# Storing x of the first three batches as one float32 plane and splitting it at its first use in the feed-forward part

## The chip, the cores and the metric

One core of a Trainium2 chip runs the whole program. The time is device microseconds of one execution. The kernel before was timed in three runs: 839.45, 842.1 and 845.86 us, median 842.1 us.

## What is computed

Attention over 4 batches, 12 heads, 448 positions and head size 64, whose scores and whose weights are mixed across the heads, and behind it a feed-forward part with a rational function:

```python
scores = scale * np.matmul(q, k.transpose(0, 1, 3, 2))
scores = np.einsum('bhij,hg->bgij', scores, w_pre)
attn = softmax(scores)
attn = np.einsum('bhij,hg->bgij', attn, w_post)
x = np.matmul(attn, v)          # as [1792 tokens, 768]
h = x @ w_in                    # w_in [768, 2048]
g = (a0 + a1*h + a2*h*h + a3*h**3) / (1 + |b0|*|h| + |b1|*h*h + 1e-6)
out = g @ w_out                 # w_out [2048, 768]
```

All inputs are float32 but for w_in and w_out, which are float64.

## The kernel before

**Attention** goes by 16 tiles of query rows, four a batch (three of 120 rows and one of 88). A tile is worked off in 6 groups (the short one in 5). For each group TensorE mixes the heads of the scores (L565, into the PSUM pair ps_t or ps_u), VectorE takes the maximum (nm, L571), ScalarE the exponential (e, L580), GpSimd and VectorE make the reciprocal of the sum (sm, rr) and GpSimd scales the second mixing matrix by it (krs, L600), TensorE mixes with that (L640, ps_a) and VectorE transposes the result (aa, L656). Between the groups TensorE makes the scores of the next tile (L496). These are copied (st, L236 on ScalarE or L238 on VectorE) and rearranged by DMA into the buffer d (L512). When all groups of a tile are through, `put_av` multiplies with v in three steps (L705) into whichever of the pairs ps_t and ps_u the groups do not use at that time; the pair is named `holds[T]`.

**What leaves attention.** After the third step, for each of the two halves hv of that pair, ScalarE copies it to Xs in the rounded matmul type (`hi`, L236, plane 0), and VectorE subtracts that from PSUM (`lo`, L723, plane 1). The two planes together carry float32 precision. The pair is free after `lo`. The planes of a batch lie in one SBUF tile `xs` (two halves, two planes, three blocks of 448 columns) and are stored to `x_scr[b]` in eight pieces (L728): four after the third tile of a batch, four after the fourth. There is one such SBUF tile, so the next batch's first `hi` waits for the stores.

**Feed-forward** goes by 64 units of one block of 128 hidden columns and one batch, in four rounds of four blocks. The first matmuls of a unit (L879, 18 of them, into ps_s) take x and the first half of W, twelve elementwise operations on ScalarE and VectorE (L892 to L929) make g, which is split in two planes (`hi` L236 or L238, `lo` L939 on GpSimd or VectorE), and 18 second matmuls (L969) add it into six PSUM banks. The float64 weights are decoded on the way (L405 to L449: ScalarE cm, GpSimd cm L415, VectorE cm and cg, ScalarE and GpSimd w L446), one piece per unit. Batches come in the order 0, 3, 1, 2 in the first round. Batch 3 is used from Xs; all others, and all later uses, are loaded from `x_scr` by `put_load_x` (L860), one DMA of 2688 KB, either into the buffer d of attention or into `xs`. The first of them (batch 0) can start when the last but one tile of attention has let go of d.

**What sets the order.** Every operation is given to `Plan` with a duration, a wished time `at` and its dependencies; `Plan.run` is a list scheduler that fixes the order of the instructions of each engine and of SP's DMA queue, and for operations that may run on two engines also which one takes it. So a change in a few operations moves many others. Each engine then works its list in order.

Of the kernel before, what the change touches and what calls it, by code (L numbers as in the profile page):

```python
# [9 lines left out]
F32 = mybir.dt.float32  # L10
F32R = mybir.dt.float32r
# [7 lines left out]
B, H, S, D = 4, 12, 448, 64  # L19
# [9 lines left out]
NT = 4 * B  # L29
# [3 lines left out]
KD = DM // 128  # L33
NF = DFF // 128
CH = 8
PH = 4
# [18 lines left out]
class Plan:  # L55
# [140 lines left out]
def dve(n, fast=False):  # L196
    return 0.16 + 0.53e-3 * n if fast else 0.14 + 1.06e-3 * n
# [14 lines left out]
ON = {  # L212
    "q_hi": ('act', 'dve'), "q_lo": ("dve", "pool"), "k_hi": ('act', 'dve'), "k_lo": ('dve', 'pool'), "w_hi": ('act',), "w_lo": ("pool",),
    "s": ('act', 'dve'), "d_hi": ('act', 'dve'), "d_lo": ("dve", "pool"), "p": ("act", "dve"), "x_hi": ("act",),
    "g_hi": ("act", "dve"), "g_lo": ("dve", "pool"),
}


def dma(nbytes):
    return nbytes / 300e3  # L220
# [21 lines left out]
def mixed_attention_then_rational_ffn(ctx: ExitStack, tc, q, k, v, w, wmix, mask, a, b2, out):  # L242
# [3 lines left out]
    nc = tc.nc  # L246
# [5 lines left out]
    add = plan.add  # L252
# [8 lines left out]
    sb = {}  # L261
# [29 lines left out]

    w_scr = [dram.tile([128, 2, WC], F32, name=f"w_scr{f}") for f in range(PH)]
    x_scr = [dram.tile([128, 2, 2, 3, S], F32, name=f"x_scr{b}") for b in range(B)]
    o_scr = [dram.tile([128, KD, S], F32, name=f"o_scr{b}") for b in range(B)]

    SLOT, HALF = 3.65, 2.2
# [2 lines left out]
    UNIT = 7.35  # L299
# [390 lines left out]
    def put_av(T, pr, at):  # L690
# [19 lines left out]
        def part(hv):  # L710
            return box[hv][:, 0:3 * n].rearrange("p (r w) -> p r w", r=3)[:, :, 0:r]

        def hi(hv):
            def fn(eng):
                if hv == 0 and T % 4 == 0:
                    Xs[b] = sb["xs"].tile([128, 2, 2, 3, S], F32R, tag="xs", name="xs")
# [20 lines left out]
        for hv in range(2):  # L737
            deps, after = [o], []
            if hv == 0 and T % 4 == 0:
                deps.append(R["xs"].take())  # L740
            else:
                after.append(xs_op[b][0])
            h_ = add(copies(3 * n, False, on=ON["x_hi"]), 0, hi(hv), deps, at=at, after=after)
            l_ = add("dve", dve(3 * n), lo(hv), [h_], at=at)
            xs_op.setdefault(b, []).append(h_)
            x_done.setdefault((b, hv), []).append(l_)
            R["ps_" + holds[T]].uses[slots[hv].k].append(l_)
            if T % 4 > 1:
                last = T % 4 == 3
                cols, done = (slice(c0, S), x_done[b, hv][3:]) if last else (slice(0, c0 + r), x_done[b, hv][:])  # L750
                for hl in range(2):
                    when = at + (3.0 if last else 5.0) + (1.6 if last else 4.0) * (2 * hl + hv)
                    s_ = bulk(0.45, store(hv, hl, cols), done, at=when, nbytes=128 * 3 * max(cols.stop - cols.start, 240) * 4, late=1.0, since=when - 1.0)
                    x_st.setdefault(b, []).append(s_)
                    R["xs"].uses[b].append(s_)

    xs_op, x_done = {}, {}
    x_st = {}

    LEAD = {1: 15.0, 2: 9.0, 3: 15.0}  # L760
    put_q(0, at=-10.0)
# [61 lines left out]
    x_use = {0: R["xs"].uses[B - 1]}  # L823
    x_ld[0] = x_done[B - 1, 0] + x_done[B - 1, 1]
    o_use, o_st = {}, {}
    m1_op = {}
# [25 lines left out]
    def put_load_x(n, at):  # L852
        b, name = homes[n]

        def fn():
# [4 lines left out]
            nc.sync.dma_start(out=t.bitcast(F32), in_=x_scr[b])  # L860
            X[n] = t
        x_ld[n] = [add(
            "sp", 0.63, fn, [R[name].take(), R["d"].uses[NT - 2] if n == 1 else op_rest, x_st[b]], at=at, extra=dma(128 * 2 * KD * S * 4))]
        x_use[n] = R[name].uses[-1]

    def put_unit(u):
        c, b, f = units[u]
# [172 lines left out]
            for c in range(NCV):  # L1040
                put_w(f, c, at=END1 - 26.0 + 6.0 * c, since=END1 - 40.0 + 6.0 * c, g=len(groups) - 8 + 2 * c)
    for n in homes:
        put_load_x(n, at=END1 + UNIT * PH * (held.index(n) - 1) + 1 if n > 1 else END1 - 45.0)
    for u in range(len(units)):
        i = u + PH * NCV
        if i < NF * NCV:
# [64 lines left out]
```

## Time and profile before

| what | value |
|---|---|
| median of three runs (lowest, highest) | 842.1 us (839.45, 845.86) |
| span of the profiled execution | 837.6 us |
| TensorE busy in the span | 802.3 us, 96% |
| VectorE, ScalarE, GpSimd busy | 684.7, 493.8, 339.4 us |
| mean granted TensorE clock | 0.994 |

The profile is of one more execution. Its span runs from the first to the last instruction; what lies around it is not shown, and the median of the timed runs stands 4.5 us above the span. Attention fills the first 350 us, the two parts overlap until about 372 us, and the rest is the feed-forward part. In the first 60 us attention starts up. Busy time of TensorE is that of its matmuls, which are pipelined; time in which it is not busy is a wait that other views put down to what ended it.

### The profile page before, as it was taken

To read this page: it belongs to the slowest core of one execution; us is meant where nothing else is said; L and a number is where in the kernel's file an instruction comes from. 1 tells how busy PE (TensorE), PEld (TensorE's weight loads), DVE (VectorE), ACT (ScalarE), POOL (GpSimd) and SP (SyncE) were. 2 spreads that over 40 slices of the span, in tenths; PEclk is the share of its full clock that TensorE was granted. 3 is DMA by queue.
4 is the path that set the end of the run, shared out by engine and by line. 5 is a ranking of instruction groups with operands and counts; after the bars stand their busy time and mean duration, and the time that the engine had idled before them with its cause. 6 is when DMAs were issued, how large, how long until landed. Compare 5 with 4: busy or idle time off the path is not lost.

```text
span 837.6 us, 23295 instructions
## 1 busy us (share of the span) xinstructions
PE 802.3 (96%) x9360; PEld 597.7 (71%) x9360; DVE 684.7 (82%) x1177; ACT 493.8 (59%) x1079; POOL 339.4 (41%) x464
## 2 busy tenths in 40 slices
PE   5789999999999999999999999999999999999998
PEld 1244454454444454589989899998999998999997
DVE  5677788788788888889988988999998999866665
ACT  2456667556565566576676665666566566445542
POOL 2224444343444343734555434465445455212111
PEclk8999999999999999999999999999999999999999
DMA  6678788677886775985633255753485544166314
GB/s 203 197 207 225 241 269 250 198 222 239 261 243 202 241 233 157 341 292 204 230 123 100 80 194 209 280 186 101 148 309 186 219 151 151 61 225 242 114 62 154
DMA packets 75355, 166.46 MB, mean 199 GB/s; under 512 B 12944, under 2 KB 52720, under 8 KB 74096
## 3 DMA queue, kind: packets, MB, share of 16 engines
q1 hardware_dynamic: 74648, 164.01, 59.1%
q8 instruction: 74, 1.21, 0.6%
q10 hardware_dynamic: 600, 0.97, 0.4%
q14 instruction: 33, 0.27, 0.1%
HBM read 88.50 MB, written 37.75 MB: 151 GB/s over the span
## 4 chain that ended last, share of the span: by engine, by line
PE 57%; DVE 16%; ACT 3%; issue 3%; POOL 2%; DMA 1%; SPq 0%; ACTq 0%; DVEq 0%; POOLq 0%
PE ps_s L879 19%; PE ps_u L969 6%; PE ps_a L969 6%; PE ps_t L969 6%; PE ps_a L640 5%; PE ps_s L496 5%; PE ps_t L565 3%; PE ps_u L705 3%; PE ps_u L565 2%; PE ps_t L705 2%; DVE cg L424 2%; DVE ua L925 2%; DVE cm L430 1%; DVE nm L571 1%; DVE ua L929 1%
## 5 line engine op out<-in xcount | busy, mean ns | idle before, releaser
L415 POOL TENSOR_SCALAR cm<-cm 128x384 f32<-128x384 f32 x64 | 103.3, 1616 | 46.6 <-ACT cm L410 46.3
L656 DVE STREAM_TRANSPOSE aa<-ps_a 128x448 f32<-128x448 f32 (+1 forms) x184 | 107.7, 617 | 13.7 <-PE ps_a L640 13.2
L939 POOL TENSOR_TENSOR g<-ua,g 128x448 fp32r<-128x448 f32 x47 | 57.8, 1230 | 138.8 <-ACT g L236 73.6
L600 POOL TENSOR_SCALAR krs<-kpost,rr 128x64 f32<-128x64 f32 x180 | 81.5, 466 | 74.3 <-DVE rr L591 54.0
L879 PE MATMUL ps_s<-xs,w 128*128 128x448 f32 x504 | 107.5, 366 | 2.9 <-DVE m L908 2.9
L879 PE MATMUL ps_s<-d,w 128*128 128x448 f32 x504 | 107.5, 366 | 1.3 <-DVE m L908 1.3
L496 PE MATMUL ps_s<-kk,q 64*64 64x448 f32 x720 | 94.4, 553 | 9.2 <-DMA kk<-in_k 5.0
L879 PEld LDWEIGHTS ps_s<-xs,w 128*128 128x128 f32 x504 | 94.4, 188 | 11.9 <-DVE m L908 4.0
L879 PEld LDWEIGHTS ps_s<-d,w 128*128 128x128 f32 x504 | 94.3, 188 | 10.3 <-DVE m L908 1.7
L236 ACT COPY st<-ps_s 120x448 f32<-120x448 f32 (+1 forms) x121 | 60.6, 533 | 68.1 <-PE ps_s L496 33.6
L640 PEld LDWEIGHTS ps_a<-e,krs 64*32 64x32 f32 x2880 | 45.2, 106 | 74.5 <-issue 34.4
L640 PE MATMUL ps_a<-e,krs 64*32 64x224 f32 x2880 | 93.6, 358 | 1.2 <-DVE aa L656 0.6
L446 POOL TENSOR_TENSOR w<-cm,w 128x384 fp32r<-128x384 f32 x48 | 54.7, 1140 | 87.7 <-ACT w L236 87.7
L892 ACT ACTIVATE m<-ps_s,a_sb 128x448 f32<-128x448 f32 x64 | 46.1, 720 | 69.5 <-PE ps_s L879 69.2
L969 PE MATMUL ps_u<-g,w 128*128 128x448 f32 x336 | 83.9, 366 | 0.0
L969 PE MATMUL ps_a<-g,w 128*128 128x448 f32 x336 | 83.8, 366 | 0.0
L969 PE MATMUL ps_t<-g,w 128*128 128x448 f32 x336 | 83.4, 366 | 0.0
L580 ACT ACTIVATE e<-ps_t,nm 128x448 f32<-128x448 f32 x92 | 57.7, 634 | 26.5 <-DVE nm L571 22.4
L587 POOL TENSOR_SCALAR sm<-sm 128x2 f32<-128x2 f32 (+1 forms) x92 | 20.9, 227 | 123.5 <-ACT e L580 121.4
L915 ACT ACTIVATE ua<-sq 128x448 f32<-128x448 f32 x64 | 37.0, 579 | 55.5 <-DVE sq L912 55.1
L580 ACT ACTIVATE e<-ps_u,nm 128x448 f32<-128x448 f32 x88 | 55.2, 634 | 24.0 <-DVE nm L571 20.4
L969 PEld LDWEIGHTS ps_t<-g,w 128*128 128x128 f32 x336 | 63.0, 188 | 5.6 <-DVE g L939 0.3
(89 smaller groups left out, 1516.5 us busy)
## 6 DMA issues: line engine op xcount, KB each, us to landing
d<-st SPq DMA_DIRECT2D x144, 210.0 KB
cr<-in_w SPq DMA_DIRECT2D x64, 384.0 KB
o_scr<-o SPq DMA_DIRECT2D x36, 448.0 KB
o<-o_scr SPq DMA_DIRECT2D x36, 448.0 KB
d<-x_scr SPq DMA_DIRECT2D x5, 2688.0 KB
xs<-x_scr SPq DMA_DIRECT2D x4, 2688.0 KB
d<-st SPq DMA_DIRECT2D x42, 157.5 KB
x_scr<-xs SPq DMA_DIRECT2D x12, 540.0 KB
```

The source lines that it names most:

```text
L236: eng.copy(o, i)
L415: nc.gpsimd.tensor_scalar(out=m, in0=m, scalar1=F64_MIN, scalar2=F64_MAX, op0=ALU.max, op1=ALU.min)
L446: eng.tensor_sub(t[:, 1, :], box["m"].bitcast(F32), t[:, 0, :].bitcast(F32))
L496: nc.tensor.matmul(box["s"][hh][i0:i1, 0:S], lhsT=Q[T][d, pr, i0:i1], rhs=K[b][d, pr, :], start=True, stop=True)
L580: nc.scalar.activation(e, box[r]["t"][:, 0:S], AF.Exp, bias=box[0]["nm"][:, r:r + 1], accum_out=box[0]["sm"][:, r:r + 1])
L600: eng.tensor_scalar_mul(box[r]["kr"], kpost, rr)
L640: nc.tensor.matmul(banks[c]["p"][q_:q_ + BT, JH * r:JH * (r + 1)], lhsT=box[r]["kr"][p, m_, :], rhs=box[r]["e"][p, JH * jh:JH * (jh + 1)], ...
L656: nc.vector.transpose(o, src)
L879: nc.tensor.matmul(h[:, 0:S], lhsT=W[fi][:, wi, kk * 128:(kk + 1) * 128], rhs=x[:, kk // 3, xj, kk % 3, :], start=(n == 0), stop=(n == 3 * ...
L892: nc.scalar.activation(new("m"), box["h"], AF.Identity, scale=a_sb[:, 3:4], bias=a_sb[:, 2:3])
L939: eng.tensor_sub(g[:, 1, :], box["rc"], g[:, 0, :].bitcast(F32))
L969: nc.tensor.matmul(O[key][:, 0:S], lhsT=W[fi][:, wi, DM + m * 128:DM + (m + 1) * 128], rhs=box["g"][:, gi, :], start=(f == 0 and n == 0), ...
```

## The change

For batches 0, 1 and 2 (`whole`), `hi` is a plain float32 copy into Y[b], one half of the same SBUF tile `xs` (the halves take turns by batch), and `lo` is gone, so that the PSUM pair is free after the copy. After the fourth tile Y is stored to a new scratch `y_scr[b]` in six pieces of 224 KB. Batch 3 stays as it was.

At the first use of batches 0, 1 and 2 in the feed-forward part `put_load_x` loads y (two DMAs of 672 KB) into the place of the second plane, ScalarE copies it block by block into the first plane (six copies of 448 columns), VectorE or GpSimd subtracts in place (six), and both planes are stored to `x_scr[b]` (two DMAs of 1344 KB) for the later uses, which load x as before.

```diff
@@ put_av
+        whole = b < B - 1
         def hi(hv):
             def fn(eng):
                 if hv == 0 and T % 4 == 0:
...
+                    if whole:
+                        Y[b] = Xs[0].rearrange("p v l k s -> p (v l) k s").bitcast(F32)[:, 2 * (b % 2):2 * (b % 2) + 2]
-                move(nc, eng, Xs[b][:, hv, 0, :, c0:c0 + r], part(hv))
+                move(nc, eng, Y[b][:, hv, :, c0:c0 + r] if whole else Xs[b][:, hv, 0, :, c0:c0 + r], part(hv))
...
+        def store_y(hv, kk):
+            def fn():
+                nc.sync.dma_start(out=y_scr[b][:, hv, kk], in_=Y[b][:, hv, kk])
+            return fn
...
-            l_ = add("dve", dve(3 * n), lo(hv), [h_], at=at)
+            l_ = h_ if whole else add("dve", dve(3 * n), lo(hv), [h_], at=at)
...
-            if T % 4 > 1:
+            if whole:
+                if T % 4 == 3:
+                    for kk in range(3):
+                        when = at + 3.0 + 1.6 * (3 * hv + kk)
+                        s_ = bulk(0.45, store_y(hv, kk), x_done[b, hv][:], at=when, nbytes=128 * S * 4, late=1.0, since=when - 1.0)
...
@@ put_load_x
+        if b in x_st:
+            x_ld[n] = [add("sp", 0.63, fn, [*free, x_st[b]], at=at, extra=dma(128 * 2 * KD * S * 4))]
+            return
...
+                nc.sync.dma_start(out=X[n][:, hv, 1].bitcast(F32), in_=y_scr[b][:, hv])
...
+                move(nc, eng, X[n][:, hv, 0, kk], X[n][:, hv, 1, kk].bitcast(F32))
...
+                x = X[n][:, hv, 1, kk]
+                eng.tensor_sub(x, x.bitcast(F32), X[n][:, hv, 0, kk].bitcast(F32))
...
+                nc.sync.dma_start(out=x_scr[b][:, hv], in_=X[n][:, hv].bitcast(F32))
...
+        for hv in range(2):
+            got.append(bulk(0.5, load(hv), [*free, y_st[b]], at=at + hv, nbytes=128 * 3 * S * 4, after=got[:1]))
...
+                h_ = add(copies(S, on=ON["x_hi"]), 0, hi(hv, kk), [got[hv]], at=when)
+                parts += [h_, add(subs(S, on=ON["x_lo"]), 0, lo(hv, kk), [h_], at=when)]
...
+            s_ = bulk(0.63, store(hv), parts, at=at + lead + gap * (3 * hv + 3) + 2.0, nbytes=128 * 2 * 3 * S * 4)
```

Three places show how the order moves. The first is VectorE at the end of a tile in attention; xs is x on its way out, rr, nm and aa belong to the groups of the next tile. Before:

```order
L591 RECIPROCAL rr<-sm 128x2
L723 TENSOR_TENSOR xs<-ps_t,xs 128x3x120 x2
L571 TENSOR_REDUCE nm<-ps_u 128x2
L656 STREAM_TRANSPOSE aa<-ps_a 128x2x7x32 x2
```

and with the change, the same place of the same tile:

```order
L592 RECIPROCAL rr<-sm 128x2
L572 TENSOR_REDUCE nm<-ps_u 128x2
L238 COPY st<-ps_s 120x448
```

The two subtractions between rr and nm are gone, and VectorE takes a copy of scores (st) behind nm; over the whole program it has 6 more of these copies than before, and ScalarE 6 fewer.

The second place is ScalarE at the end of attention, from the last copy co of the weights' decoding to the load of the table for the feed-forward part; d is where batch 0 is loaded to. Before:

```order
L236 CAST co<-cm 128x384
L580 ACTIVATE e,sm<-ps_u,nm 128x448 x2
L580 ACTIVATE e,sm<-ps_t,nm 128x448 x2
L580 ACTIVATE e,sm<-ps_u,nm 128x448 x2
L410 ACTIVATE cm<-cr 128x384
L236 CAST w_6258<-cm 128x384
L580 ACTIVATE e,sm<-ps_t,nm 128x448 x2
L236 CAST w_6258<-cm 128x384
L580 ACTIVATE e,sm<-ps_t,nm 128x448 x2
```

and with the change:

```order
L236 CAST co<-cm 128x384
L581 ACTIVATE e,sm<-ps_u,nm 128x448 x2
L236 CAST d<-d 128x448
L581 ACTIVATE e,sm<-ps_t,nm 128x448 x2
L236 CAST d<-d 128x448
L581 ACTIVATE e,sm<-ps_u,nm 128x448 x2
L236 CAST d<-d 128x448
L236 CAST w_6212<-cm 128x384
L411 ACTIVATE cm<-cr 128x384
L236 CAST d<-d 128x448 x2
L581 ACTIVATE e,sm<-ps_t,nm 128x448 x2
L236 CAST d<-d 128x448
```

The six copies of batch 0 stand one by one between the exponentials. The six subtractions behind them stand three on GpSimd, between its sm and krs, and three on VectorE, between two nm.

The third place is SP's queue in the first round of the feed-forward part, between the loads of batch 1 (into d) and of batch 2 (into xs); cr are loads of weights to decode, o_scr stores of partial sums. Before:

```order
L860 DMA d<-x_scr_123 128x5376
L405 DMA cr<-in_w 128x768 x3
L1013 DMA o_scr_126<-o 128x896 x2
L405 DMA cr<-in_w 128x768
L1013 DMA o_scr_126<-o 128x896
L405 DMA cr<-in_w 128x768
L860 DMA xs<-x_scr_124 128x5376
```

and with the change:

```order
L897 DMA d<-y_scr_127 128x1344 x2
L406 DMA cr<-in_w 128x768 x2
L1077 DMA o_scr_129<-o 128x896
L406 DMA cr<-in_w 128x768
L913 DMA x_scr_123<-d 128x2688
L1077 DMA o_scr_129<-o 128x896
L897 DMA xs<-y_scr_128 128x1344
L1077 DMA o_scr_129<-o 128x896
L406 DMA cr<-in_w 128x768
L913 DMA x_scr_123<-d 128x2688
```

The stores of the split planes, which wait for the subtractions, now stand ahead of loads of weights and of the second load of batch 2. Over the feed-forward part and the end of attention VectorE has 7 of the 18 new subtractions and GpSimd 11; besides, 9 copies and 9 subtractions of g go from VectorE to ScalarE and GpSimd. TensorE's list is the same up to the first units of the feed-forward part, and in the first round the first matmuls of batch 1 stand some groups earlier among the second ones.

## Rows read from the trace of the kernel before

**Rows 1.** Busy time by stage: PE, PEld, DVE, ACT, POOL, clock, DMA, GB/s.
```profile
60.00:350.00 290.00, 278.50 (x6100) 141.87 (x6100) 237.56 (x439) 180.30 (x483) 125.32 (x275) 0.99 0.76 235
...
372.00:480.00 108.00, 106.13 (x518) 96.72 (x517) 100.22 (x168) 75.84 (x144) 54.42 (x40) 1.00 0.45 153
480.00:720.00 240.00, 237.62 (x1167) 218.75 (x1167) 219.52 (x358) 147.18 (x275) 118.66 (x89) 1.00 0.52 186
```
**Rows 2.** Four stretches of attention, columns as in rows 1.
```profile
147.00:153.00 6.00, 5.84 (x69) 1.99 (x70) 3.60 (x6) 1.77 (x5) 1.13 (x4) 0.72 0.67 201
...
204.00:210.00 6.00, 4.52 (x128) 2.35 (x106) 4.59 (x9) 3.85 (x11) 1.45 (x4) 1.00 0.83 271
210.00:213.00 3.00, 2.28 (x44) 1.09 (x48) 1.37 (x3) 0.93 (x4) 1.72 (x2) 1.00 0.99 321
...
291.00:294.00 3.00, 1.67 (x29) 0.66 (x20) 1.24 (x5) 1.82 (x6) 0.59 (x2) 1.00 0.92 287
```
**Rows 3.** Waits of TensorE from 60 to 350: total, times, longest.
```profile
PE ps_u L565 <- DMA d<-st: 3.9, 2, 2.0
...
PE ps_t L705 <- issue: 1.3, 1, 1.3
PE ps_t L565 <- DVE xs L723: 0.6, 1, 0.6
...
PE ps_u L565 <- DVE xs L723: 0.5, 1, 0.5
```
**Rows 4.** The chain that ended last, 190 to 192: start, us, what.
```profile
190.96 0.89 DVE xs L723 x2
```
**Rows 5.** Timeline of SP's queue, two stores of x: start, us, instruction.
```profile
205.50 1.96 SPq L728 DMA_DIRECT2D x_scr<-xs  x2
...
289.74 0.76 SPq L728 DMA_DIRECT2D x_scr<-xs  x1
```
**Rows 6.** VectorE's subtraction L723 (ns min/median/max) and its wait for the copy.
```profile
L723 DVE TENSOR_TENSOR xs<-ps_u,xs x18: 409/522/533, 59.5 to 371.6; 128x360 fp32r<-128x360 f32 x12, 128x264 fp32r<-128x264 f32 x6
...
  ACT xs L236: 11.3, 12
```
**Rows 7.** Groups from 372 to 720: count, busy us, mean ns, idle before.
```profile
L939 POOL TENSOR_TENSOR g<-ua,g 128x448 fp32r<-128x448 f32 x32 | 39.8, 1244 | 49.1 <-ACT g L236 24.6 <-DVE g L238 24.6
L925 DVE SCALAR_TENSOR_TENSOR ua<-sq,ua 128x448 f32<-128x448 f32 x48 | 38.9, 810 | 0.8
...
L905 DVE TENSOR_TENSOR m<-m,ps_s 128x448 f32<-128x448 f32 x48 | 29.4, 612 | 3.9 <-ACT ua L898 3.9
...
L236 ACT CAST g<-ua 128x448 fp32r<-128x448 f32 x26 | 14.8, 569 | 14.3 <-DVE ua L929 13.2 <-PE ps_a L969 0.7
...
L939 DVE TENSOR_TENSOR g<-ua,g 128x448 fp32r<-128x448 f32 x17 | 11.2, 659 | 0.2
```
**Rows 8.** Timeline at the end of attention: start, us, instruction, idle before.
```profile
335.31 0.37 SPq L860 DMA_DIRECT2D d<-x_scr  x1
...
342.58 0.54 ACT L410 ACTIVATE cm<-cr 128x384 f32<-128x384 f32 x1
...
343.70 0.51 ACT L236 CAST w<-cm 128x384 fp32r<-128x384 f32 x1 [0.58 <-DVE cm L430]
...
344.76 0.64 ACT L580 ACTIVATE e<-ps_t,nm 128x448 f32<-128x448 f32 x1 [0.55 <-DVE nm L571]
...
346.16 1.65 PE L565 MATMUL ps_t<-d,kpre 64*64 64x448 f32 x8 [0.30 <-ACT e L580]
...
350.39 3.94 PE L879 MATMUL ps_s<-d,w 128*128 128x448 f32 x18
```
**Rows 9.** The line L925 by itself: ns min/median/max.
```profile
L925 DVE SCALAR_TENSOR_TENSOR ua<-sq,ua x64: 608/625/1466, 364.5 to 824.6; 128x448 f32<-128x448 f32 x64
```
**Rows 10.** Waits of TensorE from 372 to the end: total, times, longest.
```profile
PE ps_s L879 <- DVE m L908: 4.2, 4, 1.6
```

More of the change, by code (lines that the diff above doesn't have):

```diff
@@ L293, in mixed_attention_then_rational_ffn @@
     x_scr = [dram.tile([128, 2, 2, 3, S], F32, name=f"x_scr{b}") for b in range(B)]
+    y_scr = [dram.tile([128, 2, 3, S], F32, name=f"y_scr{b}") for b in range(B - 1)]
     o_scr = [dram.tile([128, KD, S], F32, name=f"o_scr{b}") for b in range(B)]
@@ L715, in fn @@
                 if hv == 0 and T % 4 == 0:
-                    Xs[b] = sb["xs"].tile([128, 2, 2, 3, S], F32R, tag="xs", name="xs")
-                move(nc, eng, Xs[b][:, hv, 0, :, c0:c0 + r], part(hv))
+                    if b == 0 or not whole:
+                        Xs[b] = sb["xs"].tile([128, 2, 2, 3, S], F32R, tag="xs", name="xs")
+                    if whole:
+                        Y[b] = Xs[0].rearrange("p v l k s -> p (v l) k s").bitcast(F32)[:, 2 * (b % 2):2 * (b % 2) + 2]
+                move(nc, eng, Y[b][:, hv, :, c0:c0 + r] if whole else Xs[b][:, hv, 0, :, c0:c0 + r], part(hv))
             return fn
@@ L739, in put_av @@
             if hv == 0 and T % 4 == 0:
-                deps.append(R["xs"].take())
+                if b == 0 or not whole:
+                    deps.append(R["xs"].take())
+                elif b > 1:
+                    deps.append(y_st[b - 2])
             else:
@@ L822, in mixed_attention_then_rational_ffn @@
     x_ld, m2_op, o_ev = {}, {}, {}
[L823 removed]
+    x_use = {0: R["xs"].uses[-1]}
     x_ld[0] = x_done[B - 1, 0] + x_done[B - 1, 1]
@@ L859, in fn, with load, hi, lo @@
                 t = sb[name].tile([128, 2, 2, 3, S], F32R, tag=name, name=name)
-            nc.sync.dma_start(out=t.bitcast(F32), in_=x_scr[b])
             X[n] = t
-        x_ld[n] = [add(
-            "sp", 0.63, fn, [R[name].take(), R["d"].uses[NT - 2] if n == 1 else op_rest, x_st[b]], at=at, extra=dma(128 * 2 * KD * S * 4))]
+        def fn():
+            home()
+            nc.sync.dma_start(out=X[n].bitcast(F32), in_=x_scr[b])
+        free = [R[name].take(), R["d"].uses[NT - 2] if n == 1 else op_rest]
         x_use[n] = R[name].uses[-1]
+        if b in x_st:
+            x_ld[n] = [add("sp", 0.63, fn, [*free, x_st[b]], at=at, extra=dma(128 * 2 * KD * S * 4))]
+            return
+        def load(hv):
+            def fn():
+                if hv == 0:
+                    home()
+                nc.sync.dma_start(out=X[n][:, hv, 1].bitcast(F32), in_=y_scr[b][:, hv])
+            return fn
+        def hi(hv, kk):
+            def fn(eng):
+                move(nc, eng, X[n][:, hv, 0, kk], X[n][:, hv, 1, kk].bitcast(F32))
+            return fn
+        def lo(hv, kk):
+            def fn(eng):
+                x = X[n][:, hv, 1, kk]
+                eng.tensor_sub(x, x.bitcast(F32), X[n][:, hv, 0, kk].bitcast(F32))
+            return fn
+        def store(hv):
+            def fn():
+                nc.sync.dma_start(out=x_scr[b][:, hv], in_=X[n][:, hv].bitcast(F32))
+            return fn
+        x_ld[n], x_st[b] = [], []
+        got = []
+        for hv in range(2):
+            got.append(bulk(0.5, load(hv), [*free, y_st[b]], at=at + hv, nbytes=128 * 3 * S * 4, after=got[:1]))
+            parts = []
+            for kk in range(3):
+                when = at + lead + gap * (3 * hv + kk)
+                h_ = add(copies(S, on=ON["x_hi"]), 0, hi(hv, kk), [got[hv]], at=when)
+                parts += [h_, add(subs(S, on=ON["x_lo"]), 0, lo(hv, kk), [h_], at=when)]
+            x_ld[n] += parts
+            s_ = bulk(0.63, store(hv), parts, at=at + lead + gap * (3 * hv + 3) + 2.0, nbytes=128 * 2 * 3 * S * 4)
+            x_st[b].append(s_)
+            x_use[n].append(s_)
     def put_unit(u):
@@ L1042, in mixed_attention_then_rational_ffn @@
     for n in homes:
-        put_load_x(n, at=END1 + UNIT * PH * (held.index(n) - 1) + 1 if n > 1 else END1 - 45.0)
+        if n == 1:
+            put_load_x(n, at=END1 - 45.0, lead=20.0, gap=2.0)
+        else:
+            put_load_x(n, at=END1 + UNIT * PH * (held.index(n) - 1) + 1, lead=6.0, gap=2.6)
     for u in range(len(units)):
```

13 lines of the change are left out of this document (8 added, 5 removed).

## The prediction

> **What bounds the kernel now.** I read the page first: TensorE is busy 96% of the span, VectorE 684.7 of 837.6 us, 82%. An average over two parts with different limits says little, so the busy times by stage come next [rows 1]. From 372 to 480 us TensorE works 106.13 of 108 us, from 480 to 720 us 237.62 of 240: the feed-forward part is at TensorE's limit, and nothing done there can win more than the small rest; it can only lose. VectorE is close behind with 100.22 of the same 108 us, so 7.8 us are free. In attention, from 60 to 350 us, TensorE works 278.50 of 290 us. The 11.5 us missing there are all that a faster attention can give back, beside a short stretch at a lower clock: from 147 to 153 us the granted clock was 0.72, behind a wait, which costs about 6 x 0.28 = 1.7 us [rows 2].
>
> Third, the list of TensorE's waits in attention [rows 3], to see which of the 11.5 us have to do with x. Two name the subtraction L723 itself, 0.6 and 0.5 us. The chain shows how: nm, then the two subtractions, then TensorE, at 190.96 us [rows 4]. The largest name the rearranging DMA d<-st, 3.9 us in two waits. One of these two lies between 204 and 213 us, where TensorE is idle 6 - 4.52 + 3 - 2.28 = 2.2 us while the DMA engines go to 0.99 of their capacity [rows 2]; stores of batch 1 are issued at 205.50 us [rows 5]. The stretch 291 to 294 us lacks 1.33 us with the DMA at 0.92 [rows 2], behind a store of batch 2 at 289.74 us [rows 5]; its wait has no releaser (issue, 1.3 [rows 3]), so that it belongs to x is a guess.
>
> **Attention with the change.** Removed are 24 of the 32 subtractions on VectorE: 18 of 360 columns and 6 of 264 at 0.52 and 0.41 us [rows 6], 11.8 us, and most of the 11.3 us in which VectorE stood waiting for the copy in front of them [rows 6]. The copy on ScalarE remains, and the PSUM pair comes free after it. Of x a batch stored four pieces of about 540 KB and four of 132 KB (by the code, 128 x 3 x 360 or 88 x 4 bytes), 2688 KB; now six of 224 KB, 1344 KB. The planner hands VectorE 6 score copies in return, some 0.6 us each (by L905, of their size [rows 7]), so it keeps about two thirds of its relief.
>
> What of it is on the path: 1.1 us of named waits, 2.2 us between 204 and 213 us, 1.33 us at 291 us, together 4.6 us. The new stores come in one run of six, right after the last tile of a batch, and may still meet some of the rearranging DMAs, so I take 4 us off. Bounds: a gain of 11.5 + 1.7 = 13 us, if every wait and the low clock go, and a loss of 6 us, if each of the three runs of stores makes a wait as long as the longest on d<-st, 2.0 us [rows 3].
>
> **The end of attention.** Six copies on ScalarE, three subtractions on GpSimd and three on VectorE are added between the load of batch 0, issued at 335.31 us before, and its first matmuls at 350.39 us [rows 8]. The nearest rows are the split of g: 0.569 us a copy, 1.244 us a subtraction on GpSimd, 0.659 us on VectorE [rows 7]; 3.4, 3.7 and 2.0 us. The load itself is halved, so data are there earlier. VectorE's three stand between two nm, where before TensorE had to come in between. On ScalarE the exponential at 344.76 us is what the mixing at 346.16 us waited for [rows 8]. From 342.58 us to it lie 2.18 us, in which now 0.54 + 0.51 us of old work and three copies, 1.7 us, must fit: 2.76, so 0.6 us late. The first copy waits for the load with the next exponential behind it, 0.4 us by estimate. One subtraction of GpSimd stands ahead of a krs that a mixing waits for, 1 us of its 1.244. The sum is 2 us, between nothing (ScalarE and GpSimd have gaps there) and 3.7 + 2.0 = 5.7 us, where all of GpSimd's and VectorE's new work is on the path. On SP the store of the first half of the split x, 1344 KB, goes ahead of weights, but the load ahead of it is 1344 KB shorter: nothing for the weights by bytes. If that cover fails, the second unit's first matmuls wait.
>
> **The first round of the feed-forward part.** Batches 1 and 2 add 12 copies on ScalarE (6.8 us; it has 32 us free from 372 to 480 us [rows 1]), 4 subtractions on VectorE (2.6 us) and 8 on GpSimd. The planner moves copies and subtractions of g off VectorE, in the first 16 units about 2 and 3 (at most 3.1 us by the rows of g), and so gives GpSimd some 5 subtractions more. These 13 are 16 us on top of its 54.42 us [rows 1], 30% more.
>
> That is not free for VectorE. L925, with both inputs in SBUF, has a median of 625 ns, but a longest of 1466 [rows 9] and from 372 to 720 us a mean of 810 [rows 7]; L905, which reads PSUM, has 612 [rows 7], and the removed L723, which reads PSUM too, never took more than 533 [rows 6]. So operations within SBUF are held up, about 0.13 us on the mean if L925 is the worst. With 30% more on GpSimd and eight such operations of VectorE a unit, 16 units lose 16 x 8 x 0.3 x 0.13 = 5 us. The Trainium skill (SBUF — State Buffer, section "Who interferes with whom") says that a VectorE instruction with two SBUF inputs and a GpSimd instruction that reads SBUF exclude each other for the whole instruction, and that one with at most one SBUF input does not contend. By that rule the change trades subtractions that nothing holds up for ones that can be held up and that hold up others; the rows agree with it.
>
> VectorE's net load there: 2.6 - 3.1 + 5 = 4.5 us of the 7.8 us free. TensorE loses 1.9 us there now, and in the whole feed-forward part 4.2 us to L908 [rows 10]. I take 1 us more; bounds zero and 10.7 us (second rival). The matmuls of batch 1 need block after block of x, so a late last block costs little. Later rounds load x as before: nothing.
>
> **Sum.** -4 + 2 + 1 = -1 us on the span of 837.6 us: 836.6. The median of the runs stands 4.5 us above that span, so I forecast 841.1 us. A measurement of this kernel can tell about 1%, 8.4 us, from no change (its three runs spread by 6.4 us): this would count as the same. The forecast's own range is 836 to 846 us.
>
> **Rivals.** First, VectorE and the DMA queue together hold up attention in more places than the waits named after x: the d<-st wait behind which the clock fell would go as well. For it: DMA at 0.76 and VectorE at 82% of the whole stretch [rows 1]. Against it: that wait is not next to stores of x in the queue, and TensorE is already at 96%. Then 10 of the 13 us come back, and the costs behind are 1 us: 842.1 - 9 = 833 us.
>
> Second, the slower one: GpSimd and VectorE in each other's way in the first round. Each of GpSimd's 13 added operations holds up one of VectorE's for 1466 - 608 = 858 ns [rows 9], 11.2 us; with the rest above 10.7 us, and as the orders are fixed the free 7.8 us lie where they do not help, as TensorE's 1.9 us show. Then -4 + 2 + 10.7 = +8.7 us: 850.8 us. It decides once VectorE's added time goes beyond what is free ahead of the matmuls that wait for L908. Against it: the mean hold is a seventh of that. This is also the time if the Trainium skill's exclusion strikes every time.
>
> Third, the relief in attention does not show: the runs of six stores, and the score copies that VectorE takes over, use it up. For it: 10 of the 11.5 us of waits are not named after x. Then +2 + 1 = +3 us: 845.1 us.
>
> **Chances.** The forecast 0.52, the first rival 0.17, the second 0.11, the third 0.20. Faster by over 1% is the first alone, 0.17; slower the second, 0.11; within 1% the other two, 0.72. The range of 833.5 to 850 us leaves out about half of each of the two outer cases.
>
> **What would show it.** Right: from 60 to the first L879 TensorE's idle time falls to about 7.5 us and no wait names xs but in batch 3; L723 appears 8 times; the first L879 comes 2 us earlier than at 350.39 us; the waits on L908 grow to about 5 us; the mean of L925 goes up a little in the first round. Wrong: a wait on the new subtractions (d or xs) ahead of L879 of more than 1 us, a wait of d<-st behind the y stores, L908 beyond 8 us, or the first L879 later than before.

## The result, and the profile after

The changed kernel takes 849.07 us (median of 15 runs, 847.08 to 857.81), the kernel before 842.43 us (15 runs, 839.45 to 854.03). The ratio is 1.0084, with a 95% interval of 1.006 to 1.0107: the change makes the kernel slower, by 6.6 us. The forecast was 841.1 us, a change too small to be told, on the faster side if any. 849.07 us lies within the range that was given, but the sign is that of the second rival, which had 850.8 us and a chance of 0.11.

The profiled execution of the changed kernel took 848.9 us with a span of 847.1 us. So 1.8 us lie around the span, not 4.5: the profile of before, with its span of 837.6 us, was of the fastest of the first three executions (839.45 us). About 3 us of the difference between the two spans, 9.5 us, come from that.

Busy time by stage, the columns as in [rows 1], which holds the same stretches of before:

```profile
60.00:350.00 290.00, 277.90 (x6096) 140.48 (x6094) 232.43 (x422) 180.22 (x486) 127.62 (x274) 0.99 0.72 219
...
372.00:480.00 108.00, 102.94 (x498) 92.77 (x498) 97.89 (x150) 77.69 (x151) 62.20 (x47) 1.00 0.53 178
480.00:720.00 240.00, 234.26 (x1147) 214.41 (x1146) 214.64 (x347) 150.87 (x283) 125.37 (x95) 1.00 0.54 189
```

TensorE was idle for 108 - 106.13 = 1.87 us in the first round of the feed-forward part and is now for 5.06; from 480 to 720 us it was 2.38 and is 5.74. VectorE's busy time falls in both stretches, so it does not look busier. GpSimd's rises by 7.8 us in the first.

TensorE's waits from 372 us to the end, which answer to [rows 10]:

```profile
PE ps_s L943 <- DVE m L972: 9.1, 9, 1.7
PE ps_t L1033 <- DVE g L1003: 0.9, 1, 0.9
PE ps_t L1033 <- POOL g L1003: 0.7, 1, 0.7
```

L972 is L908 of before, the last operation that reads ps_s. It was waited for 4 times, 4.2 us; now 9 times, 9.1 us. Two short waits for g are new. 6.5 us of the feed-forward part's loss stand in these three lines.

The groups from 372 to 720 us, for [rows 7] (L1003 was L939, L989 was L925, L969 was L905, and L908 are the new subtractions):

```profile
L1003 POOL TENSOR_TENSOR g<-ua,g 128x448 fp32r<-128x448 f32 x39 | 48.6, 1245 | 59.2 <-ACT g L236 37.7 <-DVE g L238 20.3 <-issue 1.2
...
L989 DVE SCALAR_TENSOR_TENSOR ua<-sq,ua 128x448 f32<-128x448 f32 x45 | 31.8, 706 | 1.4
...
L969 DVE TENSOR_TENSOR m<-m,ps_s 128x448 f32<-128x448 f32 x46 | 28.2, 613 | 3.3 <-ACT ua L962 3.1
...
L1003 DVE TENSOR_TENSOR g<-ua,g 128x448 fp32r<-128x448 f32 x8 | 6.9, 864 | 0.2 <-ACT g L236 0.2
L908 POOL TENSOR_TENSOR d<-d 128x448 fp32r<-128x448 f32 x5 | 6.8, 1368 | 0.1
L908 POOL TENSOR_TENSOR xs<-xs 128x448 fp32r<-128x448 f32 x3 | 3.8, 1279 | 1.8 <-ACT xs L236 1.8
L908 DVE TENSOR_TENSOR xs<-xs 128x448 fp32r<-128x448 f32 x3 | 2.7, 896 | 0.0
```

The eight subtractions of GpSimd for batches 1 and 2 take 1368 (five into d) and 1279 ns (three into xs) in the mean. Those on VectorE take 896 ns, not the 659 that the prediction used. The mean of L989, the line that the prediction watched, falls from 810 to 706 ns over this stretch. In the first round alone, 362 to 480 us, it rises a little, from 698 to 732 ns, as was forecast; most time is added there to L976, which was L912, 13.8 us against 10.1.

The end of attention, for [rows 8]:

```profile
341.72 1.52 POOL L908 TENSOR_TENSOR d<-d 128x448 fp32r<-128x448 f32 x1
...
342.58 0.56 ACT L236 CAST d<-d 128x448 fp32r<-128x448 f32 x1
...
343.22 0.75 POOL L601 TENSOR_SCALAR krs<-kpost,rr 128x64 f32<-128x64 f32 x1
...
343.69 0.51 ACT L236 CAST w<-cm 128x384 fp32r<-128x384 f32 x1 [0.54 <-DVE cm L431]
...
344.02 1.89 PE L641 MATMUL ps_a<-e,krs 64*32 64x224 f32 x32 [1.82 <-POOL krs L601]
...
344.39 1.07 DVE L572 TENSOR_REDUCE nm<-ps_t 128x2 f32<-128x896 f32 x1
344.57 1.02 ACT L236 CAST d<-d 128x448 fp32r<-128x448 f32 x2
...
345.56 0.64 ACT L581 ACTIVATE e<-ps_t,nm 128x448 f32<-128x448 f32 x1
...
351.71 1.08 PE L943 MATMUL ps_s<-d,w 128*128 128x448 f32 x4
```

Before, the maximum that this exponential needs:

```profile
343.59 1.07 DVE L571 TENSOR_REDUCE nm<-ps_t 128x2 f32<-128x896 f32 x1
```

Up to the maximum (nm) at 340.18 us the two profiles stand at the same time to 0.01 us. The exponential that started at 344.76 us now starts at 345.56, 0.8 us late, and the first matmuls of the feed-forward part 1.3 us. Two delays end at that exponential at the same time. Three copies of x stand ahead of it on ScalarE, the last of them done at 345.59 us. And its maximum is itself 0.8 us late: a subtraction on GpSimd, 1.52 us, stands ahead of krs, TensorE waits 1.82 us for krs, and the maximum follows. Behind that wait the granted clock of TensorE was 0.51 from 344.4 to 347.9 us, 1.2 in place of 2.4 GHz.

### The profile page after: what moved, and what is told of

The parts are those of the page before. It is cut to its first block, busy times and chain, and to the rows that moved or that the text cites. A ratio compares the mean times of both kernels' runs of the same rounds, so it can differ in the third digit from the quotient of the medians.

```text
span 847.1 us, 23309 instructions
## 1 busy us (share of the span) xinstructions
PE 807.4 (95%) x9360; PEld 596.9 (70%) x9360; DVE 684.6 (81%) x1149; ACT 502.8 (59%) x1099; POOL 363.9 (43%) x484
## 4 chain that ended last, share of the span: by engine, by line
PE 28%; DVE 25%; ACT 5%; issue 4%; POOL 2%; DMA 1%; DVEq 0%; ACTq 0%; POOLq 0%
PE ps_s L943 11%; PE ps_t L1033 4%; PE ps_u L1033 4%; PE ps_a L1033 4%; DVE cg L425 3%; DVE sq L986 3%; DVE ua L989 3%; DVE sq L976 3%; DVE m L972 2%; DVE cm L431 2%; DVE m L969 2%; DVE ua L993 2%; DVE o L1070 2%; PE ps_a L641 2%; ACT ua L983 1%
## 5 line engine op out<-in xcount | busy, mean ns | idle before, releaser
L1003 POOL TENSOR_TENSOR g<-ua,g 128x448 fp32r<-128x448 f32 x56 | 69.2, 1236 | 151.0 <-ACT g L236 87.1
L416 POOL TENSOR_SCALAR cm<-cm 128x384 f32<-128x384 f32 x64 | 102.0, 1594 | 43.4 <-ACT cm L411 43.3
L236 ACT COPY st<-ps_s 120x448 f32<-120x448 f32 (+1 forms) x115 | 58.3, 533 | 79.3 <-PE ps_s L497 40.3
L447 POOL TENSOR_TENSOR w<-cm,w 128x384 fp32r<-128x384 f32 x48 | 54.5, 1136 | 67.4 <-ACT w L236 66.2
L986 DVE TENSOR_TENSOR sq<-sq,ua 128x448 f32<-128x448 f32 x64 | 46.2, 722 | 36.2 <-ACT ua L983 36.2
```

The costliest lines, as they stand in the source:

```text
L416: nc.gpsimd.tensor_scalar(out=m, in0=m, scalar1=F64_MIN, scalar2=F64_MAX, op0=ALU.max, op1=ALU.min)
L447: eng.tensor_sub(t[:, 1, :], box["m"].bitcast(F32), t[:, 0, :].bitcast(F32))
L986: nc.vector.tensor_mul(box["vv"], box["vv"], box["rc"])
L1003: eng.tensor_sub(g[:, 1, :], box["rc"], g[:, 0, :].bitcast(F32))
```

## The experiments

Two theories were to be told apart. **W**: the added work loses the time, and in it GpSimd's subtractions, which hold VectorE up. **O**: the new order loses it; the scheduler has dealt the copies and subtractions of g anew in all rounds, and units follow each other otherwise. To hold the one while the other is changed, most of these kernels replace the scheduler by a table of its result, so that operations keep their order and engine:

```diff
-        for op in plan.run():
+        for op in table_of_order(plan.ops):
```

The feed-forward part is compared by one stretch, from VectorE's first operation on unit 0 (L969, m) to the end of the span. It has the same 2461 matmuls in each of the lines that follow. It differs by 0.05 us between two executions of the kernel before, and by 0.6 us between the changed kernel and the fourth, whose feed-forward parts have the same order; so it can be read far more finely than the timed runs, which spread by 6 us and more.

### 1 to 4: work against order, and the two halves

1: all of the change's work, in the order of before. 2: the work of before, in the order of the changed kernel (`whole = False`). 3: attention's half alone. 4: the other half alone.

```diff
 (3)
-            nc.sync.dma_start(out=X[n].bitcast(F32), in_=x_scr[b])
+            src = x_scr[b] if b == B - 1 else y_scr[b].unsqueeze(2).to_broadcast([128, 2, 2, 3, S])
+            nc.sync.dma_start(out=X[n].bitcast(F32), in_=src)
 (4)
-        whole = b < B - 1
+        whole = False
-                nc.sync.dma_start(out=X[n][:, hv, 1].bitcast(F32), in_=y_scr[b][:, hv])
+                nc.sync.dma_start(out=X[n][:, hv, 1].bitcast(F32), in_=x_scr[b][:, hv, 0])
-                nc.sync.dma_start(out=x_scr[b][:, hv], in_=X[n][:, hv].bitcast(F32))
+                nc.sync.dma_start(out=z_scr[b][:, hv], in_=X[n][:, hv].bitcast(F32))
```

> All of the change's operations, but every operation that both kernels have is issued in the order and on the engine of the kernel before (a table of the order in place of the list scheduler); the new stores, loads, copies and subtractions stand where the changed kernel has them. Theory W (the added work loses the time: the split of batches 1 and 2 in the first round of the feed-forward part, held up by GpSimd and VectorE in each other's way): as slow as the changed kernel, 847 to 851 us, and TensorE's waits on m behind 372 us about 9 us. Theory O (the new order loses it: the scheduler has dealt the copies and subtractions of g anew, in all rounds): 838 to 843 us, waits on m 4 to 6 us, and none of them longer after 480 us than before.

> The work of the kernel before (two planes from attention, no split later), in the order and on the engines of the changed kernel; the subtractions and stores of x in attention stand where the kernel before has them. Theory W: 841 to 844 us, waits of TensorE on m as before, about 4 us. Theory O: 846 to 850 us, waits on m about 8 us, half of them after 480 us. If both have a share, between the two.

> Only the half of the change that lies in attention: one float32 plane of batches 0 to 2, stored once, no subtraction there; the split is left out, and the feed-forward part loads the one plane into the place of both planes, in the order of the kernel before. It shows what attention gives back. Both theories: 4 us less than before, 837 to 840 us, with the feed-forward part as before. If the gain seen in the profile between 60 and 320 us (4.2 us) is chance: 842 us.

> Only the other half: attention stores two planes as before, and the first use in the feed-forward part loads plane 0 alone, splits it in place (plane 1 of attention's result is left out) and stores both planes to a scratch of their own; order of the changed kernel. If the halves add: the changed kernel's time plus the 4 us of attention, 851 to 855 us. If the loss needs attention's part, under 849 us.

Measured, with before at 843.54 us in the same runs: 849.48 us (1.0084, 1.0049 to 1.012), 849.82 us (1.008, 1.0047 to 1.0113), 842.89 us (0.9998, 0.9973 to 1.0023) and 856.41 us (1.0166, 1.0129 to 1.0203). By the times alone both theories are right at once, which their sum of 6.6 us doesn't allow. The feed-forward stretch parts them. It is shown for before, 2, 3, 4 and the changed kernel:

```profile
360.82:837.60 476.78, 468.60 (x2461) 430.10 (x2459) 405.17 (x668) 283.90 (x525) 193.87 (x145) 1.00 0.49 173
```
```profile
369.06:847.40 478.34, 468.93 (x2461) 429.97 (x2459) 399.57 (x651) 287.89 (x532) 202.08 (x153) 1.00 0.49 172
```
```profile
367.87:845.20 477.33, 468.68 (x2461) 430.07 (x2459) 405.35 (x668) 283.91 (x525) 194.01 (x145) 1.00 0.49 173
```
```profile
370.83:855.20 484.37, 470.43 (x2461) 429.56 (x2459) 407.96 (x655) 293.07 (x544) 213.00 (x161) 1.00 0.51 179
```
```profile
362.12:847.10 484.98, 470.43 (x2461) 429.53 (x2459) 408.02 (x655) 293.01 (x544) 212.53 (x161) 1.00 0.51 179
```

The change adds 485.0 - 476.8 = 8.2 us there. The new order by itself adds 1.6 us (478.34). With the split it is 484.4 to 485.0, whatever attention did. So the split work adds 6.0 to 6.6 us, and theory W holds for the feed-forward part. The halves don't simply add: the fourth kernel came out 1.4 us above its range. In the second kernel TensorE's waits on m from 372 us on are 5.8 us, between the 4 of theory W and the 8 of theory O. Some 4.7 of the 6.3 us by which it is slower must lie ahead of the feed-forward part; its single profile doesn't say where. From the tenth to the eighty-first maximum of attention it takes 264.1 us and the fourth kernel 266.0, against 260.8 in the first profile of before and 263.8 in its second (below). Both kernels give VectorE the subtractions of x back in an order that was made without them; that this is what costs there is likely, but not shown.

The first kernel's stretch is 483.6 us; its clock was 0.97 between 372 and 480 us behind waits, and 3.6 of its 6.9 us are slower matmuls (472.2 us of busy time against 468.6), so it says less of order. Its time, as slow as the changed kernel, is what theory W expected; its waits on m, 5.1 us, are not (about 9), they lie in the range of theory O. From 480 to 720 us TensorE is idle for 2.38 us in it, exactly as in before, where the changed kernel has 5.74: what is lost in the later rounds goes with the new order.

The third kernel missed the 4 us that both theories expected: attention's half, in the order of before, gives nothing (the interval reaches from 2.3 us faster to 1.9 us slower). Its time is the one expected for the case that the gain seen in the profile is chance, 842 us.

### 5 to 7: which subtractions

These keep the order of the changed kernel and leave out, of the twelve subtractions of batches 1 and 2, all, the four on VectorE, or the eight on GpSimd (in the table these entries are dropped).

> The changed kernel in its own order, but the twelve subtractions of batches 1 and 2 are left out (plane 1 stays the whole value); loads, copies and stores stay. Theory S (the subtractions cost the 6 to 8 us, since VectorE is the engine that sets the pace of the first round): 842 to 844 us, first round (first m of unit 0 to that of unit 16) 114 us in place of 120.5, the time in which VectorE's operations take longer than their shortest about 18 us there in place of 23. Rival C (the copies on ScalarE, late for the logarithm and exponential that VectorE waits for, and the transfers): 847 to 850 us, first round 118 to 120 us.

> The same with only VectorE's four of these left out. Theory S by load alone: 4 x 0.89 us = 3.5 us off the first round, 845 to 846 us. If GpSimd's eight carry the cost by holding VectorE up: at most 2 us off, 847 to 849 us, and the excess of VectorE stays at 22 to 23 us.

> The same with only GpSimd's eight left out. If they cost by holding VectorE up: the excess falls from 23 to 18 us, the first round by 4 to 5 us, 844 to 845 us, although GpSimd's own time is not what anything waits for. If the load of VectorE is the cost: excess may fall, but the first round by under 2 us, 847 to 849 us.

Measured, with before at 843.06 us: 844.03 us (1.0019, 0.999 to 1.0047), 849.54 us (1.0118, 1.0062 to 1.0173) and 844.44 us (1.003, 1.0004 to 1.0055). Without VectorE's four nothing is won; without GpSimd's eight nearly all is. The feed-forward stretch of the three, in the same order:

```profile
361.70:841.50 479.80, 469.36 (x2461) 429.86 (x2459) 398.86 (x651) 292.84 (x544) 203.43 (x153) 1.00 0.51 181
```
```profile
361.46:846.00 484.54, 470.35 (x2461) 429.55 (x2459) 404.60 (x651) 292.96 (x544) 212.11 (x161) 1.00 0.51 180
```
```profile
366.37:845.80 479.43, 468.85 (x2461) 429.86 (x2459) 402.20 (x655) 292.66 (x544) 202.02 (x153) 1.00 0.51 181
```

What the first round shows of the kernels with the changed kernel's order (first m of unit 0 to that of unit 16, and in it the sum by which VectorE's operations run longer than the shortest of their form, both worked out from the timeline):

| kernel | first round, us | VectorE's excess, us |
|---|---|---|
| changed | 120.5 | 23.2 |
| 2, work of before | 114.5 | 17.7 |
| 5, no subtractions | 115.7 | 17.0 |
| 6, none on VectorE | 120.5 | 22.9 |
| 7, none on GpSimd | 115.1 | 18.2 |
| 9, memsets for them (below) | 116.4 | 19.6 |
| 10, on VectorE (below) | 118.6 | 18.5 |

GpSimd's eight are worth 484.98 - 479.43 = 5.55 us, VectorE's four 0.4 us, which is within what the stretch differs by itself: with the eight gone, dropping the four as well makes it no shorter (479.80). What stays with all twelve gone, 479.80 against 478.34, is 1.5 us, left for the copies and the transfers, which no run took out by themselves. GpSimd has 63.22 us of work from the first m to 480 us, 118 us, so it is not short of time.

TensorE's waits from 350 to 480 us show most of it. The changed kernel has three on m and the two on g that were shown above, 4.9 us; without the eight one on m is left. Changed kernel, then the seventh:

```profile
PE ps_s L943 <- DVE m L972: 3.3, 3, 1.5
```
```profile
PE ps_s L943 <- DVE m L972: 1.1, 1, 1.1
```

How eight operations of an engine with time to spare take 5.6 us shows in the timeline of VectorE and GpSimd, changed kernel:

```profile
396.13 1.16 POOL L908 TENSOR_TENSOR d<-d 128x448 fp32r<-128x448 f32 x1
396.58 0.92 DVE L420 TENSOR_SCALAR cm<-cm 128x384 int32<-128x384 int32 x1
397.24 1.14 POOL L447 TENSOR_TENSOR w<-cm,w 128x384 fp32r<-128x384 f32 x1
397.42 1.44 DVE L1003 TENSOR_TENSOR g<-ua,g 128x448 fp32r<-128x448 f32 x1
398.34 1.54 POOL L908 TENSOR_TENSOR d<-d 128x448 fp32r<-128x448 f32 x1
398.78 1.51 DVE L425 SCALAR_TENSOR_TENSOR cg<-cr,cm 128x384 int32<-128x384 int32 x1
400.22 0.61 DVE L238 COPY o<-ps_t 128x448 f32<-128x448 f32 x1
...
401.75 0.67 DVE L972 SCALAR_TENSOR_TENSOR m<-m,a_sb,ps_s 128x448 f32<-128x448 f32 x1
...
402.47 0.87 PE L943 MATMUL ps_s<-xs,d 128*128 128x448 f32 x3 [1.07 <-DVE m L972]
```

Elsewhere L420 takes 0.36 us, L1003 0.61 and L425 0.55. Here each ends only 0.2 to 0.5 us after the operation of GpSimd beside it has ended: L420 is 0.56 us late and L425 0.96 us, both behind L908. Operations that read PSUM are not held: in the whole feed-forward part L972 takes 0.67 us in the mean, both beside an operation of GpSimd and with none beside it. Three holds in a row bring L972 late, and TensorE waits 1.07 us for it. VectorE's excess can be put to the GpSimd operation that overlaps most with the one held (holds over 0.1 us, from the timeline): L908 has 5.6 us, L447 6.7, L1003 5.2, L416 3.3. Without the eight, the other three have the same (6.8, 5.2, 3.1). So the eight hold VectorE by some 0.7 us each, 5.6 us together, and the stretch is longer by as much.

### 8: attention's half, rescheduled

The code of the third experiment with the scheduler left in.

> Attention's half alone as in the third experiment, but in the order that the list scheduler makes for it. That experiment kept the order of before and gave nothing (842.9 against 843.5 us). If the relief of attention needs a new order (score copies dealt to VectorE, groups earlier): 838 to 840 us, from the tenth to the eighty-first maximum 257 us as in the changed kernel. If the 4 us in the changed kernel's profile are chance: 842 to 844 us and 260 us or more.

Measured: 843.31 us (1.0, 0.9969 to 1.0031), the time of the second answer, and 259.8 us between the two maxima, 0.2 us short of it. Its feed-forward part, in an order of its own, is some us longer (its stretch begins at another matmul, so that it can't be compared), so the time may hide what attention gave; the relief is not shown here.

### 9 and 10: what holds, and another place for it

```diff
 (9)
+                if n > 1 and eng is nc.gpsimd:
+                    for _ in range(3):
+                        nc.gpsimd.memset(junk, 0.0)
+                    return
                 x = X[n][:, hv, 1, kk]
                 eng.tensor_sub(x, x.bitcast(F32), X[n][:, hv, 0, kk].bitcast(F32))
```

The tenth has no edit in the functions: in the table of the order the eight entries name VectorE.

> The changed kernel in its own order; in place of each of GpSimd's eight subtractions of batches 1 and 2 it sets a spare tile of 128x448 to zero three times, about as long, and reads nothing (these subtractions are left out). If VectorE is held up by GpSimd's reading of SBUF: as without the eight, 844 to 845 us, excess of VectorE in the first round 18 us, first round 115 us, no operation of VectorE held while a memset runs. If it is the time on GpSimd that makes its other work late (w, g): 848 to 850 us, first round 120 us.

> The changed kernel in its own order with the eight subtractions moved from GpSimd to VectorE, at the same places; the result is the whole one. The hold measured with them was 5 us, 0.6 us for one; a subtraction on VectorE takes 0.61 us where nothing holds it. If that is the price: the same as the changed kernel within 1.5 us, 847.5 to 850.5 us, excess 18 to 19 us. If GpSimd is the dearer place, because a hold hits operations that TensorE waits for: 844 to 847 us.

Measured, with before at 843.07 us: 846.03 us (1.003, 1.0002 to 1.0058), 1 us above what was expected, and 847.11 us (1.0039, 1.0021 to 1.0057). The stretches:

```profile
358.98:839.70 480.72, 469.55 (x2461) 429.71 (x2459) 403.44 (x655) 293.01 (x544) 213.06 (x177) 1.00 0.52 181
```
```profile
360.33:843.00 482.67, 470.10 (x2461) 429.52 (x2459) 406.35 (x663) 293.06 (x544) 204.38 (x153) 1.00 0.51 180
```

With the memsets GpSimd is as busy as in the changed kernel (213.06 against 212.53 us), but the stretch is 1.3 us longer than without the eight, not 5.55. Beside a memset VectorE's operations with two inputs in SBUF run unhindered, beside a subtraction they don't. VectorE and GpSimd of the ninth kernel (L982 was L976, L422 was L420, L449 was L447):

```profile
397.69 0.95 DVE L982 TENSOR_TENSOR sq<-sq,ua 128x448 f32<-128x448 f32 x1
...
399.09 0.61 DVE L982 TENSOR_TENSOR sq<-sq,ua 128x448 f32<-128x448 f32 x1
...
402.93 0.60 DVE L422 TENSOR_SCALAR cm<-cm 128x384 int32<-128x384 int32 x1 [1.38 <-POOL cm L418]
```
```profile
395.64 1.53 POOL L911 MEMSET junk<- 128x448 f32 x3
397.13 1.03 POOL L449 TENSOR_TENSOR w<-cm,w 128x384 fp32r<-128x384 f32 x1
398.10 1.54 POOL L911 MEMSET junk<- 128x448 f32 x3
...
402.84 1.63 POOL L911 MEMSET junk<- 128x448 f32 x3
```

L982 at 397.69 us is held until L449 ends; the next, at 399.09, has only memsets beside it and takes its 0.61 us. The holds that fall to memsets sum to 1.4 us, those of the subtractions in their place to 5.6. The 1.4 us are five holds. Two of them, 0.7 us, are of operations that began beside L449, which reads, and ended behind it, as at 397.69 us. The other three, 0.7 us, are of L422, which has one input in SBUF, as at 402.93 us; the last section comes back to it. No operation with two inputs was held by a memset alone. This is what the Trainium skill states (SBUF — State Buffer, section "Who interferes with whom"): a VectorE instruction with two SBUF inputs contends with a GpSimd instruction that reads SBUF, not with one that only writes it. The runs agree.

On VectorE the same eight subtractions cost 482.67 - 479.43 = 3.2 us, 0.4 us each, against 0.7 us on GpSimd. 847.11 us lies between the two answers, but the stretch is 2.3 us shorter than in the changed kernel: the expectation that the two prices are equal was wrong. VectorE is the cheaper place, and that kernel is 2 us faster than the changed one, still slower than before.

### 11 and 12: a smaller change, and before once more

```diff
 (11)
-        whole = b < B - 1
+        whole = b < 1
```

(with the buffer of xs taken anew for each other batch, as before).

> A version that may beat both: only batch 0, whose split lies at the end of attention, leaves as one plane; batches 1 to 3 go as before. The list scheduler makes its order. Attention keeps a third of the relief, 0 to 1 us, the end loses about 1 us, no subtraction falls in the first round: 842 to 845 us, no gain over before that could be told.

> The kernel before once more, for a profile of an ordinary execution: the one that the prediction was read from had 839.4 us, the lowest of its runs. If TensorE's clock in the first 60 us is what executions differ in, as the profile of the changed kernel suggests (0.79 from 36 to 60 us against 1.00): a span of about 841 us whose first ten maxima end 2 to 4 us later than in that profile, and all behind as there. Feed-forward part from the first m to the end 477 us.

Measured: 842.29 us (0.9979, 0.9957 to 1.0002) and 844.49 us (1.0013, 0.9988 to 1.0038). With batch 0 alone nothing can be told from no change; no version here beats both for certain. The repeat of before gives attention's scatter. The stretch from the tenth to the eighty-first maximum, in before's first profile, its second, the changed kernel and the third experiment:

```profile
54.50:315.25 260.75, 249.01 (x5463) 127.40 (x5459) 209.09 (x388) 160.47 (x430) 107.10 (x236) 0.99 0.77 235
```
```profile
56.74:320.52 263.78, 249.61 (x5462) 127.14 (x5461) 209.56 (x387) 160.18 (x430) 106.89 (x236) 0.99 0.75 232
```
```profile
58.47:315.26 256.79, 247.22 (x5463) 125.37 (x5459) 203.63 (x370) 157.10 (x424) 106.73 (x236) 1.00 0.73 222
```
```profile
58.52:322.29 263.77, 250.85 (x5461) 127.79 (x5453) 200.09 (x363) 159.69 (x430) 107.36 (x236) 0.99 0.71 216
```

Six profiles have the changed kernel's attention in its own order (it and experiments 5, 6, 7, 9 and 10): 254.2 to 261.6 us, 257.2 in the mean, 5 us under the mean of the two of before. With the same relief in the old order (1 and 3) it is 261.2 and 263.8: none. So the gain seems to need the order that the scheduler makes from the relief; with profiles that lie up to 7 us apart in one order, and 261.6 us for one of the six, it is not shown beyond doubt. The tenth maximum starts at 56.6 to 58.8 us in those six, at 54.5 and 56.7 in before; whether this is the change or chance stays open. Of the repeat's expectation the feed-forward stretch came out (476.73 us) and the first stage too (2.2 us later), but attention behind it did not stand as in the first profile: it took 3.0 us more, and the span was 843.1 us, not about 841.

## Why the prediction was wrong

**Attention, -4 us: right in sign, its size not settled.** The profiles have 5 us less in the mean from the tenth to the eighty-first maximum, but the tenth itself is 2.4 us later in the mean, so that the eighty-first comes only 2.7 us earlier. The named places were right in part: in the changed kernel's profile no wait names the subtraction of x, and none d<-st. But d<-st is back in four of the five other profiles of its order, 1.3 to 1.5 us, and TensorE now has waits named after the stores of y (y_scr<-xs, 1.3 us, and 0.5 to 0.9 in those five) and after one of weights (w_scr<-co, 2.4 us). TensorE's idle time from 60 us to the first matmuls did not fall to 7.5 us: it is 12.1 us against 11.5. Between the two maxima it is 9.6 us against 11.7 and 14.2 in the two profiles of before, and the stretch at the low clock, 0.72 from 147 to 153 us [rows 2], is gone: the changed kernel had 1.00 there, and of the six profiles only that of experiment 7 has such a stretch between the two maxima. The sum took the relief to be worth 4 us in any order; the third experiment refutes that.

**End of attention, +2 us: nearly right.** In profiles of the changed kernel's order the stage from the eighty-first maximum to the first m takes 46.2 to 47.1 us against 45.6 and 45.9: about 1 us. The sum added 0.6 us for the copies on ScalarE, 0.4 for the first of them and 1 for the subtraction ahead of krs. The first of them made no exponential late, and the other two run side by side, so that together they cost the exponential 0.8 us; in all six profiles TensorE waits 1.8 us for krs. The clock was not in the sum: where it fell behind that wait (the changed kernel, 5 and 7) the stage takes 46.9 to 47.1 us, where it did not (6, 9 and 10) 46.2.

**First round, +1 us: the term that failed.** It measured 8.2 us over the whole feed-forward part: 1.6 for the new order, 1.5 for copies and transfers, 0.4 for VectorE's four subtractions in the full kernel, and the rest, 4.7 us, for GpSimd's eight, which gave back 5.55 when they alone were taken out. The size of the hold was near: the step "16 units lose 16 x 8 x 0.3 x 0.13 = 5 us" stands against 5.6 us from the first m of unit 0 to that of unit 16, where VectorE's excess over its shortest durations rises from 17.6 to 23.2 us. The step that failed is the next: "VectorE's net load there: 2.6 - 3.1 + 5 = 4.5 us of the 7.8 us free", and from it "I take 1 us more". The 7.8 us are gaps, and by the groups of before most of them lie in front of L922 and L905, which wait for ScalarE (5.6 and 1.2 us from 362 to 480 us); in front of L908 (now L972), the operation that is late, there is 0.1 us, so they cover nothing. Before, from 362 to 480 us (behind the bars: busy us and mean ns, then the idle time ahead):

```profile
L908 DVE SCALAR_TENSOR_TENSOR m<-m,a_sb,ps_s 128x448 f32<-128x448 f32 x17 | 11.4, 671 | 0.1
...
L922 DVE TENSOR_TENSOR sq<-sq,ua 128x448 f32<-128x448 f32 x17 | 11.1, 650 | 5.6 <-ACT ua L919 5.6
...
L905 DVE TENSOR_TENSOR m<-m,ps_s 128x448 f32<-128x448 f32 x16 | 9.8, 612 | 1.2 <-ACT ua L898 1.2
```

The kernel's own rows said so: with 7% of VectorE free TensorE waited for L908 already [rows 10]. The eight's holds of 5.6 us came out as 5.55 us of time: nothing of them was covered. The second rival said this ("the free 7.8 us lie where they do not help") and came within 2 us of the time, in part by luck: its price per operation, 0.858 us, was high by a fifth, eight, not 13, of the added operations carried the cost, and of the 8.2 us 1.6 come from the order, in which it saw no cost. Two of the signs that were to show the forecast wrong came: the waits on L908 (now L972) are 9.1 us, beyond 8, and the first matmuls of the feed-forward part come later than before.

**Later rounds, nothing: wrong.** The scheduler dealt copies and subtractions of g anew in all rounds, and TensorE's waits from 480 to 720 us rose from 2.4 to 5.7 us; in the second experiment, with the new order and without any split, they are 5.4, in the first, with the split and the old order, 2.4. From 372 to 480 us the second kernel waits 0.4 us, less than the 1.9 of before; over the whole stretch that leaves the 1.6 us of the order, which are counted above.

**The offset of 4.5 us** was taken for what lies around the span. It is 1.8 us; the rest was that the profiled execution was a fast one. The error did not touch the sum, which was made against the same span.

The timed sum by these: +8.2 in the feed-forward part, and 849.07 - 842.43 - 8.2 = -1.6 us in all that lies ahead of it, where -4 + 2 = -2 was forecast.

## What to carry to other kernels

Work that is handed to an engine with time to spare is not free if the two engines cannot run beside each other: price it by what it does to the busy engine's operations (here 0.7 us for each GpSimd subtraction, against 0.4 us on VectorE itself), and check whether the gaps of that engine lie ahead of the operation that the bound engine waits for. Free time as an average over a stage covers nothing by itself. And where a scheduler makes the order, keep its order fixed while work is changed, and the work fixed while order is changed, before a difference is put down to either.

## What the runs showed that was not expected

Not only operations with two inputs in SBUF are held up: L420, with one input, takes 0.36 us alone and 1.30 us beside GpSimd's L908, which ran from 407.81 to 408.95 us:

```profile
407.87 1.30 DVE L420 TENSOR_SCALAR cm<-cm 128x384 int32<-128x384 int32 x1 [0.54 <-POOL cm L416]
```

In the ninth experiment the same operation, L422 there, takes 0.51 to 0.60 us three times beside memsets, which read nothing, and 0.35 us a fourth time. The prediction took from the Trainium skill (SBUF — State Buffer, section "Who interferes with whom") that an instruction with at most one SBUF input does not contend; the page says this only of instructions outside VectorE's 2-port modes, and the prediction left the condition out. Whether L420 runs in such a mode no run shows.

And TensorE's clock differs between executions with the same order: from 36 to 60 us, behind a wait for vv (in experiment 10 for d<-st), the mean of the granted clock was 0.79 in the changed kernel and in experiments 5 and 9, and 0.93 in 6, 7 and 10; before had 1.00 and, repeated, 0.93. Those below 1.00 are means over parts at 2.4 and parts at 1.2 GHz. A single profile of attention is good to some 4 us only; that of the feed-forward part agreed to 0.05 us in the one kernel that was profiled twice, where TensorE's clock stood at 1.00 in both.
